# Linear attention feeding a two-layer network on one core: the opening reordered, and the attention of batches 3 to 7 computed with tokens on partitions and transposed by DMA

## The chip, the cores and the metric

The kernel runs on one core of a Trainium2 chip. The metric is device time in microseconds (us), the median of several executions. A profiled execution has a "span", which is about 1.7 us shorter than its time. Engines: PE is TensorE's matmul, PEld its weight load, DVE VectorE, ACT ScalarE, POOL GpSimd, SP SyncE; SPq is a DMA issue on SP. PSUM is the memory that matmuls write their results to; "regrouped" means copied so that all heads of a token lie together.

## The reference

```python
kv  = einsum('bhsd,bhse->bhde', k, v)            # 8 batches, 8 heads, 576 tokens, head size 64
out = einsum('bhsd,bhde->bhse', q, kv)
rms = sqrt(mean(out * out, axis=-1, keepdims=True) + 1e-6)
x   = (out / rms * g_norm)                       # -> 4608 tokens x 512
h   = x @ w_in                                   # 512 x 2048
g   = maximum(h, 0) + alpha * minimum(h, 0)
y   = g @ w_out                                  # 2048 x 512, float32 out
```

## The kernel before

The 4608 tokens are processed in nine windows of 512. The kernel keeps x transposed (features on partitions, tokens in columns), because the first layer needs it so. For each batch and pair of heads j, four small steps make it: transposing q on TensorE, kv, ot, and the norm with a sum over partitions made by a matmul with a mask.

```python
def step_t(b, j, pool=(ps_s, "s")):
    qs = bufs[b % NBUF]["q"]                      # q regrouped to tokens x heads
    qt_ps = pool[0].tile([P, NT * P], FP16, name="qt_ps", tag=pool[1])
    for t in range(NT):
        nc.tensor.matmul(out=qt_ps[:, t * P:(t + 1) * P], lhsT=qs[:, t, 2 * j:2 * j + 2, :],
                         rhs=ident16[:], is_transpose=True, ...)
    ...
def step_ot(w, j):      # ot_ps[features of the pair, 512 tokens] = kv^T q^T; then ACT squares it
def step_ssq(w, j):
    ot_ps, sq = ots.pop((w, j))
    ssq_ps = ps_q.tile([P, W], FP32, name="ssq_ps", tag="q")
    nc.tensor.matmul(out=ssq_ps[:], lhsT=mask16[:], rhs=sq[:], start=True, stop=True)
    # ACT: rstd = exp(-0.5 * ln(ssq / 64 + eps)), two passes of 128x512
    # DVE: xt = ot_ps * g * rstd
```

A window runs its first layer in 16 groups of four matmuls. Four second-layer matmuls of the window before follow each group, and then attention steps of the window after, spread over the groups:

```python
for w in range(1, NW):
    steps = window_steps(w + 1) if w + 1 < NW else []
    ...
    if 1 < w and w + 2 < B:
        load_batch(w + 2)                         # POOL issues six DMAs, fp32 to fp16
        regroup_batch(w + 2)                      # POOL copies to tokens x heads
    for g in range(NF):
        ...
        m1_group(w, g)                            # four matmuls h, then ACT Relu, DVE gt
        ...                                       # four matmuls y of window w - 1
        want = n * (g - first_g + 1) // (NF - 2 - first_g)
        while steps and n - len(steps) < want:
            steps.pop(0)()
```

Everything is scheduled by hand: each engine executes its instructions in the order in which this program emits them. That includes SP, which issues DMAs.

## Time and profile before

| | before |
|---|---|
| time | 329.71 us median (329.23 to 330.53) |
| span | 328.0 us |
| first first-layer matmul of window 2 | 90.0 us |
| from there to the end | 238.0 us |
| DMA packets under 512 B | 14,304 |

The clock row, the DMA totals, the queue that SP issues on, and the output stores are in the page of before (packets, MB, share of 16 engines; for the issue the last number is the median us to landing):

```profile
PEclk9999999798999999999999999999999999999999
...
DMA packets 47621, 28.07 MB, mean 86 GB/s; under 512 B 14304, under 2 KB 42992, under 8 KB 47600
...
q1 hardware_dynamic: 5696, 9.45, 10.2%
...
out_dram<-y_sb SPq DMA_DIRECT2D x40, 128.0 KB, 2.3
```

The clock is full after slice 10 (each slice is 8.2 us), and SP's queue carries little besides the output, 9.44 MB.

### The profile page before, as it was taken

The page shows a single profiled execution, that of the slowest core. Times are in us where ns is not written, and L with a number is a line of the kernel's source. Part 1 is how long each engine was busy: PE and PEld are TensorE (multiplying, and loading weights), DVE is VectorE, ACT ScalarE, POOL GpSimd, SP SyncE. Part 2 cuts the span into 40 slices and gives each one's busy share as a digit, 9 for nine tenths or more (in the row PEclk, how much of TensorE's full clock was granted, in tenths as well). Part 3 has the DMA queues.
Part 4 walks back from the last instruction along what each step waited for, and adds up shares of the span by engine and source line. Part 5 has one row for each costly group of instructions (what it writes and reads, how often), then busy time and mean ns, then how long its engine had stood idle before and what let it go on. Part 6 is the DMA issues. An engine that isn't in the chain of part 4 may idle for free.

```text
span 328.0 us, 4205 instructions
## 1 busy us (share of the span) xinstructions
PE 298.4 (91%) x1593; PEld 143.7 (44%) x1593; DVE 160.2 (49%) x271; ACT 173.4 (53%) x291; POOL 74.7 (23%) x80
## 2 busy tenths in 40 slices
PE   5657998768799999999999999999999999999994
PEld 1323354234355545544555455445544444444441
DVE  4247833285665545555455545554555455444300
ACT  2366605635846564657456745674557576544311
POOL 9723442765542055105500000000000000000000
PEclk9999999798999999999999999999999999999999
DMA  7999999996391199109901111101000211000132
GB/s 95 193 203 202 198 195 191 223 145 83 38 178 33 34 126 154 34 33 149 134 32 34 32 32 34 51 13 53 36 23 21 59 38 34 32 32 34 44 86 64
DMA packets 47621, 28.07 MB, mean 86 GB/s; under 512 B 14304, under 2 KB 42992, under 8 KB 47600
## 3 DMA queue, kind: packets, MB, share of 16 engines
q0 software_dynamic: 41904, 18.35, 44.5%
q1 hardware_dynamic: 5696, 9.45, 10.2%
q8 instruction: 12, 0.20, 0.3%
q14 instruction: 9, 0.07, 0.1%
HBM read 36.71 MB, written 9.44 MB: 141 GB/s over the span
## 4 chain that ended last, share of the span: by engine, by line
PE 83%; ACT 7%; DVE 4%; DMA 2%; issue 1%; POOL 1%; POOLq 0%; ACTq 0%
PE h_ps L300 36%; PE y_ps L322 34%; PE kv_ps L237 3%; PE ssq_ps L268 2%; PE qt_ps L222 2%; PE ot_ps L256 2%; ACT rstd L270 2%; DMA qsb<-in_q_dram 2%; ACT rstd L273 2%; DVE xt L275 1%; DVE gt L309 1%; ACT sq_sb L262 1%; ACT m_sb L307 1%; PE yd L322 1%; DVE qt_sb L231 1%
## 5 line engine op out<-in xcount | busy, mean ns | idle before, releaser
L300 PE MATMUL h_ps<-xt,w_in_sb 128*128 128x512 f16 x576 | 147.3, 384 | 4.1 <-ACT y_sb L329 1.5
L309 DVE SCALAR_TENSOR_TENSOR gt<-m_sb,beta_sb,h_ps 128x512 f16<-128x512 f32 x144 | 106.8, 745 | 88.4 <-ACT m_sb L307 86.9
L307 ACT ACTIVATE m_sb<-h_ps 128x512 f32<-128x512 f32 x144 | 85.1, 593 | 83.7 <-PE h_ps L300 83.6
L322 PE MATMUL y_ps<-w_out_sb,gt 128*128 128x512 f16 x512 | 128.8, 379 | 0.0
L322 PEld LDWEIGHTS <-gt 128*128 128x128 f16 x576 | 56.0, 98 | 67.5 <-issue 2.3
L300 PEld LDWEIGHTS <-w_in_sb 128*128 128x128 f16 x576 | 54.9, 99 | 67.2 <-issue 14.5
L275 DVE SCALAR_TENSOR_TENSOR xt<-ot_ps,g2col,rstd 128x512 f16<-128x512 f32 x36 | 27.0, 751 | 46.5 <-ACT rstd L273 46.5
L270 ACT ACTIVATE rstd<-ssq_ps,eps_t 128x512 f32<-128x512 f32 x36 | 24.7, 686 | 18.2 <-PE ssq_ps L268 18.2
L262 ACT ACTIVATE sq_sb<-ot_ps 128x512 f16<-128x512 f32 x36 | 21.3, 597 | 22.6 <-PE ot_ps L256 22.1
L329 ACT COPY y_sb<-y_ps 128x512 f32<-128x512 f32 x32 | 18.7, 585 | 18.4 <-PE y_ps L322 18.4
L273 ACT ACTIVATE rstd<-rstd 128x512 f32<-128x512 f32 x36 | 22.7, 629 | 1.1
L268 PE MATMUL ssq_ps<-sq_sb,mask 128*128 128x512 f16 x36 | 13.6, 378 | 7.0 <-ACT sq_sb L262 5.5
L222 PE MATMUL qt_ps<-ident,qsb 128*128 128x128 f16 x160 | 14.8, 227 | 5.7 <-DVE qsb L139 4.8
L237 PE MATMUL kv_ps<-vsb,ksb 128*128 128x128 f16 x160 | 14.5, 226 | 4.7 <-DVE qt_sb L231 4.7
L222 PEld LDWEIGHTS <-qsb 128*128 128x128 f16 x160 | 11.8, 101 | 13.5 <-DVE qsb L139 5.9
L231 DVE COPY qt_sb<-qt_ps 128x576 f16<-128x576 f16 x32 | 14.3, 451 | 6.4 <-PE qt_ps L222 6.3
L237 PEld LDWEIGHTS <-ksb 128*128 128x128 f16 x160 | 11.9, 101 | 12.1 <-issue 6.1
L256 PE MATMUL ot_ps<-qt_sb,kv_sb 128*128 128x512 f16 (+7 forms) x64 | 14.2, 296 | 0.3 <-DVE kv_sb L245 0.3
L128 POOL DMA_DIRECT2D ksb<-in_k_dram x8 | 5.6, 700 | 36.4 <-PE kv_ps L237 27.8
L139 POOL COPY ksb<-kst 128x2048 f16<-128x2048 f16 x5 | 9.5, 1893 | 18.7 <-DMA kst<-in_k_dram 18.7
L139 POOL COPY qsb<-qst 128x2048 f16<-128x2048 f16 x5 | 9.5, 1894 | 7.4 <-DMA qst<-in_q_dram 7.4
L139 POOL COPY vsb<-vst 128x2048 f16<-128x2048 f16 x5 | 9.5, 1894 | 6.8 <-DMA vst<-in_v_dram 6.8
(44 smaller groups left out, 111.6 us busy)
## 6 DMA issues: line engine op xcount, KB each, us to landing
out_dram<-y_sb SPq DMA_DIRECT2D x40, 128.0 KB, 2.3
out_dram<-y_sb SPq DMA_DIRECT2D x16, 256.0 KB, 2.3
kst<-in_k_dram POOLq DMA_DIRECT2D x7, 512.0 KB, 8.6
vst<-in_v_dram POOLq DMA_DIRECT2D x7, 512.0 KB, 10.1
qst<-in_q_dram POOLq DMA_DIRECT2D x7, 512.0 KB, 12.0
w_in_sb<-in_moe_w_in_dram POOLq DMA_DIRECT2D x4, 512.0 KB, 10.9
w_out_sb<-in_moe_w_out_dram POOLq DMA_DIRECT2D x4, 512.0 KB, 16.5
kst<-in_k_dram POOLq DMA_DIRECT2D x2, 256.0 KB, 5.5
```

The lines of the kernel that those rows point to most:

```text
L139: (eng or nc.vector).tensor_copy(out=dst, in_=src)
L222: nc.tensor.matmul(out=qt_ps[:, t * P : (t + 1) * P], lhsT=qs[:, t, 2 * j : 2 * j + 2, :], rhs=ident16[:], is_transpose=True, start=(t == ...
L237: nc.tensor.matmul(out=kv_ps[:], lhsT=ks[:, t, 2 * j : 2 * j + 2, :], rhs=vs[:, t, 2 * j : 2 * j + 2, :], start=(t == 0), stop=(t == NT - 1),)
L256: nc.tensor.matmul(out=ot_ps[:, n0 - w * W : n1 - w * W], lhsT=kvs[b, j][:], rhs=qts[b, j][:, n0 - b * S : n1 - b * S], start=True, stop=True,
L262: nc.scalar.activation(out=sq[:], in_=ot_ps[:], func=AF.Square)
L270: nc.scalar.activation(out=rstd[:], in_=ssq_ps[:], func=AF.Ln, bias=eps_t[:], scale=inv_d,)
L273: nc.scalar.activation(out=rstd[:], in_=rstd[:], func=AF.Exp, bias=0.0, scale=-0.5)
L275: nc.vector.scalar_tensor_tensor(out=xts[w, j][:], in0=ot_ps[:], scalar=g2col[:], in1=rstd[:], op0=ALU.mult, op1=ALU.mult,)
L300: nc.tensor.matmul(out=h_ps[:], lhsT=w_in_blk(c, g), rhs=xts[w, c][:], start=(c == 0), stop=(c == NC - 1),)
L307: nc.scalar.activation(out=m_sb[:], in_=h_ps[:], func=AF.Relu, scale=-1.0)
L309: nc.vector.scalar_tensor_tensor(out=gt[:], in0=m_sb[:], scalar=beta_sb[:, g : g + 1], in1=h_ps[:], op0=ALU.mult, op1=ALU.add,)
L322: nc.tensor.matmul(out=y[:], lhsT=gts[w, g][:, a * P : (a + 1) * P], rhs=w_out_blk(g), start=(g == 0), stop=(g == NF - 1),)
```

## The change

The intent has two parts. Part 1 shortens the opening: v is used as it was loaded instead of being regrouped, the loads and copies of batch 0 are reordered, and window 1's attention starts earlier. Part 2 takes work off TensorE from batch 3 on: a DMA transposes q straight from the regrouped buffer, a tile of 128 tokens times all eight heads is computed with tokens on partitions (so that the norm is a short VectorE reduction), and a second DMA transposes the finished x rows. The core of the diff:

```diff
+    NB_PE = 3
@@ part 1 (cut)
+    for nm, src in (("q", q), ("k", k), ("v", v)):           # remainder of batch 0, now on SP
+        nc.sync.dma_start(out=rem0[nm][0:REM], in_=src[0, :, MAIN:S, :]...)
     alpha_row = ...; nc.sync.dma_start(out=alpha_row[:], ...)
-        for nm in ("k", "v", "q"):
+        for nm in ("k", "q"):
             regroup(b, nm, 0, H, nc.gpsimd)
+            if nm == "v" and t < TPP:
+                return stages[b, nm][:, 2 * j : 2 * j + 2, t, :]
@@ part 2
+    def transpose_q(b):
+        qtms[b] = attn_p.tile([P, NT * NPAIR, P], FP16, name="qtm")
+        nc.sync.dma_start_transpose(out=qtms[b][:], in_=bufs[b % NBUF]["q"][:]...)
+    def tile_a(b, t):      # 4 matmuls of 128 columns: otm_ps = q kv; ACT squares
+        ot_ps = ps_o.tile([P, H, D], FP32, name="otm_ps", tag=f"o{n_tile[0] % 3}")
+    def tile_b(b, t):      # DVE sums over each head
+    def tile_c(b, t):      # ACT ln, exp on 128x8; POOL rg = rstd * g
+    def tile_d(b, t):
+        nc.vector.tensor_mul(out=x[0:n], in0=ot_ps[0:n], in1=rg[0:n])
+        nc.sync.dma_start_transpose(out=xm(w)[:, :, c : c + m], in_=x[i : i + m]...)
@@ the window loop
+            if g == NF - 3 and max(w + 2, NB_PE) < B and w + 2 >= NB_PE:
+                transpose_q(w + 2)

             want = n * (g - first_g + 1) // (NF - 2 - first_g)
             while steps and n - len(steps) < want:      # the last tile_d's come out of here
```

At group 13 of a window, q's transpose for the batch after next is therefore emitted just ahead of the tiles' last steps, on the same queue.

More of the change, by code (lines that the diff above doesn't have):

```diff
@@ L48 @@
     inv_d = 1.0 / D
+    NB_PE = 3
     const_p = ctx.enter_context(tc.tile_pool(name="constp", bufs=1))
     w_p = ctx.enter_context(tc.tile_pool(name="weights", bufs=1))
-    xt_p = ctx.enter_context(tc.tile_pool(name="xt", bufs=3))
+    xt_p = ctx.enter_context(tc.tile_pool(name="xt", bufs=2))
+    xm_p = ctx.enter_context(tc.tile_pool(name="xm", bufs=3))
     qkv_p = ctx.enter_context(tc.tile_pool(name="qkv", bufs=1))
@@ L60 @@
     ps_s = ctx.enter_context(tc.tile_pool(name="pss", bufs=1, space=bass.MemoryType.PSUM))
-    ps_o = ctx.enter_context(tc.tile_pool(name="pso", bufs=2, space=bass.MemoryType.PSUM))
-    ps_q = ctx.enter_context(tc.tile_pool(name="psq", bufs=1, space=bass.MemoryType.PSUM))
+    ps_o = ctx.enter_context(tc.tile_pool(name="pso", bufs=1, space=bass.MemoryType.PSUM))
     ctx.enter_context(
@@ L95 @@
     nc.vector.memset(warm16[:], 0.5)
+    rem0 = {}
+    for nm, src in (("q", q), ("k", k), ("v", v)):
+        rem0[nm] = ysb_p.tile([P, H, D], FP32, name=f"rem0{nm}", tag="y_sb")
+        nc.sync.dma_start(
+            out=rem0[nm][0:REM], in_=src[0, :, MAIN:S, :].rearrange("h s d -> s h d"),
+        )
     alpha_row = const_p.tile([NF, P], FP32, name="alpha_row")
     nc.sync.dma_start(out=alpha_row[:], in_=moe_alpha[:].rearrange("(g p) -> g p", p=P))
+    g_all = const_p.tile([P, D], FP32, name="g_all")
+    nc.sync.dma_start(out=g_all[:], in_=g_norm[:].partition_broadcast(P))
     g2col = const_p.tile([P, 1], FP32, name="g2col")
@@ L111 @@
         for nm in ("k", "v", "q"):
-            t[nm] = qkv_p.tile([P, NT, H, D], FP16, name=f"{nm}sb{i}")
-            nc.vector.memset(t[nm][REM:P, TPP, :, :], 0.0)
+            n = 1 if nm == "v" else NT
+            t[nm] = qkv_p.tile([P, n, H, D], FP16, name=f"{nm}sb{i}")
+            nc.vector.memset(t[nm][REM:P, n - 1, :, :], 0.0)
         bufs.append(t)
@@ L128, in load_rem @@
         nc.gpsimd.dma_start(
-            out=bufs[b % NBUF][nm][0:REM, TPP, :, :],
+            out=bufs[b % NBUF][nm][0:REM, 0 if nm == "v" else TPP, :, :],
             in_=srcs[nm][b, :, MAIN:S, :].rearrange("h s d -> s h d"),
@@ L179, in w_out_blk @@
         return w_out_sb[i][:, r, :]
-    for nm in ("k", "v", "q"):
-        load_main(0, nm, 0, H // 2)
-    for nm in ("k", "v", "q"):
-        load_rem(0, nm)
-    for nm in ("k", "v", "q"):
-        load_main(0, nm, H // 2, H)
+    for h0 in (0, H // 2):
+        for nm in ("q", "k", "v"):
+            load_main(0, nm, h0, h0 + H // 2)
     for i in range(WQ):
         load_w_in(i)
-    load_batch(1, ("k",))
+    load_batch(1, ("k", "q"))
     load_w_out(0)
-    load_w_out(1)
-    load_batch(1, ("v", "q"))
-    load_w_out(2)
-    load_w_out(3)
+    load_batch(1, ("v",))
+    for i in range(1, WQ):
+        load_w_out(i)
     load_batch(2)
     def keep_warm(n):
-        ps = ps_y.tile([P, W], FP32, name="warm_ps", tag="y")
+        ps = ps_s.tile([P, W], FP32, name="warm_ps", tag="s")
         for i in range(n):
@@ L216, with pair_cols, f @@
     qts, kvs, xts = {}, {}, {}
+    def pair_cols(b, nm, j):
+        def f(t):
+            if nm == "v" and t < TPP:
+                return stages[b, nm][:, 2 * j : 2 * j + 2, t, :]
+            if nm == "v":
+                return bufs[b % NBUF][nm][:, 0, 2 * j : 2 * j + 2, :]
+            return bufs[b % NBUF][nm][:, t, 2 * j : 2 * j + 2, :]
+        return f
     def step_t(b, j, pool=(ps_s, "s")):
-        qs = bufs[b % NBUF]["q"]
+        qs = pair_cols(b, "q", j)
         qt_ps = pool[0].tile([P, NT * P], FP16, name="qt_ps", tag=pool[1])
@@ L223, in step_t @@
                 out=qt_ps[:, t * P : (t + 1) * P],
-                lhsT=qs[:, t, 2 * j : 2 * j + 2, :],
+                lhsT=qs(t),
                 rhs=ident16[:],
@@ L233, in step_kv @@
     def step_kv(b, j, pool=(ps_s, "s")):
-        ks, vs = bufs[b % NBUF]["k"], bufs[b % NBUF]["v"]
+        ks, vs = pair_cols(b, "k", j), pair_cols(b, "v", j)
         kv_ps = pool[0].tile([P, P], FP32, name="kv_ps", tag=pool[1])
@@ L238, in step_kv @@
                 out=kv_ps[:],
-                lhsT=ks[:, t, 2 * j : 2 * j + 2, :],
-                rhs=vs[:, t, 2 * j : 2 * j + 2, :],
+                lhsT=ks(t),
+                rhs=vs(t),
                 start=(t == 0),
@@ L248, with xt_of, step_ot @@
     ots = {}
-    def step_ot(w, j):
-        ot_ps = ps_o.tile([P, W], FP32, name="ot_ps", tag="o")
+    xms = {}
+    def xt_of(w, c):
+        return xms[w][:, c, :] if w >= NB_PE else xts[w, c][:]
+    def step_ot(w, j, pool=None):
+        if pool is not None:
+            ot_ps = pool[0].tile([P, W], FP32, name="ot_ps", tag=pool[1])
+        else:
+            ot_ps = ps_o.tile([P, W], FP32, name="ot_ps", tag=f"o{j % 2}")
         n0 = w * W
@@ L265, in step_ssq, with ssq_mm @@
     def step_ssq(w, j):
+        ssq_mm(w, j)
+        norm(w, j)
+    def ssq_mm(w, j):
         ot_ps, sq = ots.pop((w, j))
-        ssq_ps = ps_q.tile([P, W], FP32, name="ssq_ps", tag="q")
+        ssq_ps = ps_o.tile([P, W], FP32, name="ssq_ps", tag="o2")
         nc.tensor.matmul(out=ssq_ps[:], lhsT=mask16[:], rhs=sq[:], start=True, stop=True)
@@ L273, in step_ssq, with norm @@
         nc.scalar.activation(out=rstd[:], in_=rstd[:], func=AF.Exp, bias=0.0, scale=-0.5)
+        ots[w, j] = (ot_ps, rstd)
+    def norm(w, j):
+        ot_ps, rstd = ots.pop((w, j))
         xts[w, j] = xt_p.tile([P, W], FP16, name="xt", tag=f"xt{j}")
@@ L278, in step_ssq, with step_tail_ot @@
         )
+    TAIL = NB_PE * (S - W)
+    JT = min(NPAIR, W // TAIL)
+    def step_tail_ot(i):
+        ot_ps = ps_o.tile([P, JT, TAIL], FP32, name="ot_ps", tag=f"o{i % 2}")
+        for u in range(JT):
+            j = i * JT + u
+            nc.tensor.matmul(
+                out=ot_ps[:, u, :], lhsT=kvs[NB_PE - 1, j][:],
+                rhs=qts[NB_PE - 1, j][:, S - TAIL : S], start=True, stop=True,
+            )
+        sq = attn_p.tile([P, JT, TAIL], FP16, name="sq_sb")
+        nc.scalar.activation(out=sq[:], in_=ot_ps[:], func=AF.Square)
+        ots["tail", i] = (ot_ps, sq)
@@ new lines, in step_tail_ssq @@
+    def step_tail_ssq(i):
+        ot_ps, sq = ots.pop(("tail", i))
+        ssq_ps = ps_o.tile([P, JT, TAIL], FP32, name="ssq_ps", tag="o2")
+        nc.tensor.matmul(out=ssq_ps[:], lhsT=mask16[:], rhs=sq[:], start=True, stop=True)
+        rstd = attn_p.tile([P, JT, TAIL], FP32, name="rstd")
+        nc.scalar.activation(
+            out=rstd[:], in_=ssq_ps[:], func=AF.Ln, bias=eps_t[:], scale=inv_d,
+        )
+        nc.scalar.activation(out=rstd[:], in_=rstd[:], func=AF.Exp, bias=0.0, scale=-0.5)
+        nc.vector.scalar_tensor_tensor(
+            out=xm(NB_PE)[:, i * JT : (i + 1) * JT, 0:TAIL], in0=ot_ps[:], scalar=g2col[:],
+            in1=rstd[:], op0=ALU.mult, op1=ALU.mult,
+        )
@@ new lines, with xm @@
+    qtms, tiles = {}, {}
+    def xm(w):
+        if w not in xms:
+            xms[w] = xm_p.tile([P, NPAIR, W], FP16, name="xm")
+        return xms[w]
+    def transpose_q(b):
+        qtms[b] = attn_p.tile([P, NT * NPAIR, P], FP16, name="qtm")
+        nc.sync.dma_start_transpose(
+            out=qtms[b][:], in_=bufs[b % NBUF]["q"][:].rearrange("p t h d -> p (t h d)"),
+        )
+    n_tile = [0]
+    def tile_a(b, t):
+        ot_ps = ps_o.tile([P, H, D], FP32, name="otm_ps", tag=f"o{n_tile[0] % 3}")
+        n_tile[0] += 1
+        for j in range(NPAIR):
+            nc.tensor.matmul(
+                out=ot_ps[:, 2 * j : 2 * j + 2, :], lhsT=qtms[b][:, t * NPAIR + j, :],
+                rhs=kvs[b, j][:], start=True, stop=True,
+            )
+        n = P if t < TPP else REM
+        sq = attn_p.tile([P, H, D], FP32, name="sqm_sb", tag="rstd")
+        nc.scalar.activation(out=sq[0:n], in_=ot_ps[0:n], func=AF.Square)
+        tiles[b, t] = [n, ot_ps, sq]
@@ new lines, in tile_b @@
+    def tile_b(b, t):
+        n, _, sq = tiles[b, t]
+        ss = attn_p.tile([P, H], FP32, name="ss", bufs=3)
+        nc.vector.tensor_reduce(
+            out=ss[0:n], in_=sq[0:n], op=ALU.add, axis=mybir.AxisListType.X,
+        )
+        tiles[b, t][2] = ss
+    def tile_c(b, t):
+        n, _, ss = tiles[b, t]
+        nc.scalar.activation(
+            out=ss[0:n], in_=ss[0:n], func=AF.Ln, bias=eps_t[0:n], scale=inv_d,
+        )
+        nc.scalar.activation(out=ss[0:n], in_=ss[0:n], func=AF.Exp, bias=0.0, scale=-0.5)
+        rg = attn_p.tile([P, H, D], FP32, name="rg")
+        nc.gpsimd.tensor_tensor(
+            out=rg[0:n], in0=ss[0:n].unsqueeze(2).to_broadcast([n, H, D]),
+            in1=g_all[0:n].unsqueeze(1).to_broadcast([n, H, D]), op=ALU.mult,
+        )
+        tiles[b, t][2] = rg
@@ new lines, in tile_d, with phase_steps @@
+    def tile_d(b, t):
+        n, ot_ps, rg = tiles.pop((b, t))
+        x = attn_p.tile([P, H, D], FP16, name="xrow", bufs=3)
+        nc.vector.tensor_mul(out=x[0:n], in0=ot_ps[0:n], in1=rg[0:n])
+        i = 0
+        while i < n:
+            w, c = divmod(b * S + t * P + i, W)
+            m = min(n - i, W - c)
+            nc.sync.dma_start_transpose(
+                out=xm(w)[:, :, c : c + m], in_=x[i : i + m].rearrange("p h d -> p (h d)"),
+            )
+            i += m
+    def phase_steps(w):
+        if w < NB_PE:
+            return window_steps(w)
+        if w >= NW:
+            return []
+        todo = [(b, t) for b in range(NB_PE, min(B, w + 1)) for t in range(NT)
+                if (b, t) not in done and b * S + t * P < (w + 1) * W]
+        done.update(todo)
+        old = [x for x in todo if x[0] < w]
+        new = [x for x in todo if x[0] == w]
+        pre = []
+        if w == NB_PE:
+            n = NPAIR // JT
+            pre = [lambda i=i: step_tail_ot(i) for i in range(n)] + [
+                lambda i=i: step_tail_ssq(i) for i in range(n)]
+        kv = [lambda j=j: step_kv(w, j) for j in range(NPAIR)] if w < B else []
+        first = []
+        for i in range(max(len(pre), len(kv))):
+            first += kv[i : i + 1] + pre[i : i + 1]
+        seq = old + new
+        lead = len(old)
+        steps = []
+        if lead == 0:
+            steps += [[f] for f in first]
+            first = []
+        for i in range(len(seq) + 3):
+            m = []
+            for k, fn in ((3, tile_d), (0, tile_a), (1, tile_b), (2, tile_c)):
+                if 0 <= i - k < len(seq):
+                    m.append(lambda fn=fn, x=seq[i - k]: fn(*x))
+            if i < lead:
+                cut = -(-len(first) // (lead - i))
+                m += first[:cut]
+                first = first[cut:]
+            steps.append(m)
+        return [lambda m=m: [f() for f in m] for m in steps]
@@ L280, in window_steps @@
+    done = set()
     def window_steps(w):
@@ L300, in m1_mm @@
             nc.tensor.matmul(
-                out=h_ps[:], lhsT=w_in_blk(c, g), rhs=xts[w, c][:],
+                out=h_ps[:], lhsT=w_in_blk(c, g), rhs=xt_of(w, c),
                 start=(c == 0), stop=(c == NC - 1),
@@ L345 @@
     H_POOL = (ps_h, "h")
-    for j0 in (0, 2):
-        regroup(0, "q", 2 * j0, 2 * j0 + 4)
-        regroup(0, "v", 2 * j0, 2 * j0 + 4, nc.scalar)
-        regroup(0, "k", 2 * j0, 2 * j0 + 4)
-        j1 = j0 + 1
-        step_t(0, j0, H_POOL)
-        step_t(0, j1, H_POOL)
-        step_kv(0, j0)
-        step_kv(0, j1, H_POOL)
-        step_ot(0, j0)
-        step_ot(0, j1)
-        if j0 == 0:
-            keep_warm(4)
-            step_ssq(0, j0)
-            step_ssq(0, j1)
-            keep_warm(6)
+    for nm in ("q", "k", "v"):
+        nc.scalar.copy(out=bufs[0][nm][0:REM, 0 if nm == "v" else TPP, :, :], in_=rem0[nm][0:REM])
+    regroup(0, "q", 0, H // 2)
+    step_t(0, 0, H_POOL)
+    regroup(0, "k", 0, H // 2)
+    step_t(0, 1, H_POOL)
+    keep_warm(3)
+    step_kv(0, 0)
+    step_kv(0, 1, H_POOL)
+    step_ot(0, 0)
+    step_ot(0, 1)
+    regroup(0, "q", H // 2, H)
+    step_t(0, 2, H_POOL)
+    regroup(0, "k", H // 2, H)
+    step_t(0, 3, H_POOL)
+    ssq_mm(0, 0)
+    ssq_mm(0, 1)
+    norm(0, 0)
+    step_kv(0, 2)
+    step_kv(0, 3, H_POOL)
+    norm(0, 1)
+    step_ot(0, 2)
+    step_ot(0, 3, (ps_y, "y"))
     first = [ps_h.tile([P, W], FP32, name="h_ps", tag="h") for g in range(3)]
@@ L365 @@
     step_ssq(0, 2)
+    keep_warm(2)
     step_ssq(0, 3)
@@ L373 @@
         m1_group(0, g)
-    for nm in ("q", "k", "v"):
-        regroup(1, nm, 0, H)
+        if g == 10:
+            regroup(1, "k", 0, H)
+        if g == 14:
+            regroup(1, "q", 0, H)
+    AHEAD = 3
     ys = [
@@ L381 @@
         ps_h.tile([P, W], FP32, name="yc", tag="h"),
-        ps_h.tile([P, W], FP32, name="yd", tag="h"),
     ]
     steps = window_steps(1)
+    n = len(steps)
     for g in range(NF):
-        for a in range(TPW):
+        for a in range(AHEAD):
             y_mm(ys[a], 0, a, g)
-            if g >= 6 and steps and (a == 1 or (a == 3 and g >= 8)):
+            if a != 1 and steps and n - len(steps) < n * (AHEAD * g + a + 1) // (AHEAD * (NF - 3)):
                 steps.pop(0)()
-    for a in range(TPW):
+    for a in range(AHEAD):
         y_out(ys[a], 0, a)
-    for f in steps:
-        f()
+    regroup_batch(2)
     for w in range(1, NW):
-        steps = window_steps(w + 1) if w + 1 < NW else []
+        steps = phase_steps(w + 1)
         n = len(steps)
@@ L404 @@
             if w == 1 and g == first_g - 1:
-                for nm in ("q", "k", "v"):
-                    regroup(2, nm, 0, H)
                 load_batch(3)
@@ L409 @@
             m1_group(w, g)
-            if w > 1:
+            if w == 1:
+                if g == 0:
+                    y = ps_y.tile([P, W], FP32, name="y_ps", tag="y")
+                y_mm(y, 0, AHEAD, g)
+                if g == NF - 1:
+                    y_out(y, 0, AHEAD)
+            else:
                 a, part = divmod(g, TPW)
```

## The prediction

> **What bounds the kernel now.** I read the summary of engines first, then the slices of the span, the busy time by stretch, TensorE's waits, and the timeline of TensorE instruction by instruction.
>
> From the page (engines, then 40 slices of 8.2 us each, tenths of busy time):
>
> ```profile
> PE 298.4 (91%) x1593; PEld 143.7 (44%) x1593; DVE 160.2 (49%) x271; ACT 173.4 (53%) x291; POOL 74.7 (23%) x80
> ...
> PE   5657998768799999999999999999999999999994
> ...
> DMA  7999999996391199109901111101000211000132
> GB/s 95 193 203 202 198 195 191 223 145 83 38 178 33 34 126 154 34 33 149 134 32 34 32 32 34 51 13 53 36 23 21 59 38 34 32 32 34 44 86 64
> ```
>
> There are two regimes. In the first eleven slices (to about 90 us) TensorE has holes and the DMA engines are full: they load weights and batches 0 to 3. After that TensorE is full and the DMA engines are mostly free. The stretches say it in microseconds (start:end, length, busy time of each engine, clock, DMA, GB/s):
>
> ```profile
> 0.00:9.87 9.87, 4.64 (x11) 1.56 (x12) 4.35 (x19) 2.33 (x2) 8.34 (x17) 1.00 0.99 106
> 9.87:39.00 29.13, 23.27 (x122) 11.21 (x123) 16.95 (x29) 16.91 (x28) 13.59 (x18) 1.00 1.38 200
> 39.00:62.40 23.40, 18.84 (x118) 9.37 (x116) 9.11 (x17) 9.11 (x17) 9.34 (x9) 1.00 1.49 190
> 62.40:90.00 27.60, 21.92 (x116) 10.43 (x116) 17.04 (x29) 16.15 (x30) 16.54 (x16) 0.88 0.77 112
> 90.00:308.50 218.50, 215.07 (x1162) 104.71 (x1161) 111.96 (x178) 125.34 (x212) 26.91 (x22) 1.00 0.32 56
> ```
>
> Busy matmul time is not work, because matmuls overlap: the timeline shows four 512-column matmuls every 0.86 us, so one costs 0.216 us of TensorE, not the 0.38 us of its row; five 128-column ones cost 0.28 us, 0.056 each:
>
> ```profile
> 93.78 0.44 PE L237 MATMUL kv_ps<-vsb,ksb 128*128 128x128 f16 x5
> 94.06 1.03 PE L300 MATMUL h_ps<-xt,w_in_sb 128*128 128x512 f16 x4
> 94.92 1.03 PE L322 MATMUL y_ps<-w_out_sb,gt 128*128 128x512 f16 x4
> 95.79 0.44 PE L222 MATMUL qt_ps<-ident,qsb 128*128 128x128 f16 x5
> ...
> 118.82 0.38 PE L268 MATMUL ssq_ps<-sq_sb,mask 128*128 128x512 f16 x1 [0.69 <-ACT sq_sb L262]
> ```
>
> With these costs, window 2 starts at 90.0 us. From there remain 448 first-layer and 512 second-layer matmuls, 960 x 0.2158 = 207.2 us; attention of batches 3 to 7 at 20 transposes, 20 kv, and 4 + 4 wide matmuls each (2 x 1.11 + 8 x 0.216 = 3.95 us), plus 1.73 for the last window: 21.5 us; five stalls like the last line (0.84 us lost each), 4.2 us; and 4.8 us after the last matmul. Sum 237.7; the trace has 238.0. So TensorE alone bounds the last 238 us. Before 90 us there are only 192 x 0.216 + 3 x 4 = 53.4 us of TensorE work: 36.6 us are lost. TensorE's waits name where:
>
> ```profile
> PE ssq_ps L268 <- ACT sq_sb L262: 5.5, 7, 1.2
> PE qt_ps L222 <- DVE qsb L139: 4.8, 3, 2.9
> PE kv_ps L237 <- DVE qt_sb L231: 4.7, 5, 1.9
> ```
>
> qsb is the regrouped q: TensorE waits for data that has landed and is being rearranged by VectorE.
>
> **What the Trainium skill says.** "VectorE: DVE Perf Modes", The three transpose paths, gives 1309 ns for one 128x128 transpose by DMA and 390 ns on TensorE. The trace puts a TensorE transpose at 0.056 us in a stream, so the move saves little per tile. "DMA: Bandwidth & Descriptors", Latency and other measured facts, gives 261 GB/s for a DMA transpose with a non-contiguous middle dimension; no transpose of this kind is in the trace. The same page, Issuing engines are not separate DMA queues, says that all queues share 16 engines; in the trace the output stores' time to landing runs from 2.0 through a median of 2.3 to 5.7 us, which fits sharing but doesn't prove it. "GPSIMD Engine Reference", 3.1, has 4497 ns for a two-input operation of 2048 elements; from it I estimate 1.2 us for the 512-element one added here; the trace has only copies (1.89 us for 2048 f16).
>
> **Part 1, the opening.** Removed: regrouping v everywhere (kv reads the staged v with strides); the remainder loads of batch 0 leave POOL's queue; the second half of q and k no longer stands behind the norm of the first half on VectorE; window 1's attention starts with the first y matmul, not at g = 6; a quarter of window 0's y moves into window 1. Working: before, the half batches have landed by 9.4 (q) and 14.9 us, yet the second half's q copy ran at 18.4 because it stood behind the norm; first-layer matmuls began at 20.9 and 26.0. Unblocked, I put those at 17.5 (w_in's first quarter landed at about 17.4, from POOL's queue waits) and 22.1: 3.5 us gained. Window 0's first layer ends at 36 instead of 39, less 0.7 for two regroupings on VectorE among its evacuations. Then y with three columns: 48 x 0.216 + 4.0 attention + 1.5 of stalls, to 52; before, four columns ended at 60.6, and the next window began at 62.5. Window 1: 80 x 0.216 + 4.0 + 3.5 of stalls = 24.8, against 27.6 before for 64. So window 2 starts at about **77.5** instead of 90.0. The bytes and their order hardly change; the arrival times of w_out (30, 31, 42, 45 us before) and of batch 2 (near 54) still fit.
>
> **Part 2, tokens on partitions, batches 3 to 7.** Removed from TensorE: 100 transposes (5.6 us), 24 wide ssq (5.2), 24 wide ot (5.2), five stalls (4.2). Added: 100 ot matmuls of 128 columns (25 tiles of 4; 5.6 us), the tail of batch 2 (0.65). kv stays. Net 238 - 14 = 223.9 us from window 2 to the end, if nothing new waits. ACT loses two passes of 0.63 to 0.69 us per pair; VectorE gains a reduction per tile; both are at half load and not the bound.
>
> What is added on the path, from the built order of instructions:
> - Three PSUM buffers hold the tiles, and the fourth tile of a window waits for tile_d of the first, which on VectorE stands behind this group's gt. From lines like those above: the group ends at 95.09, Relu to 95.72, gt to 96.50, tile_d 0.7 more to 97.2, while TensorE is ready at 95.79: 1.4 us. Windows with 4, 5, 4, 5, 4 tiles have 1 + 2 + 1 + 2 + 1 = 7 such waits: **9.8 us**.
> - The next window's first matmul needs all its xm. The last tile_d ends 2.1 us after group 13's end, and TensorE arrives 4.15 us after it. A transpose DMA as quick as the stores (2.3) lands at 4.4: 0.3 us, six times. But the q transpose (655 KB; 2.5 us at 261 GB/s, an estimate from that page) stands just before it in SP's queue in four windows; in two of them it is issued one group later, and x waits 1.2. Sum **3.5 us** if the page's rate holds. If it runs twice as long, these four lose 3 to 5 us each: about 20 us.
> - POOL's product stands behind the load and regrouping of a batch (14.3 + 1.9 us, from 64.68 to 80.8): free 11 to 14 us into a window, needed at 13 to 14. **1 us**.
>
> Sum with the quick transposes: 77.5 + 223.9 + 14.3 = 315.7 us of span, 317.4 with the 1.7 us between span and time. With slow ones about 332.
>
> **The rivals.** (1) The transposes are hidden and only the opening and 14 us of TensorE work count: 77.5 + 223.9 + 1.7 = 303; against it are the built order's waits, which I don't see how to avoid. (2) The DMA transpose takes the bound: 1309 ns each one after the other would be 26 us for 20 tiles, over 50 us per batch with x, more than a window's 32 us; then time goes above 345. For it: no trace of this case shows its speed; against: the page's rate. (3) The wait moves from regrouped q to DMA arrival in the opening, and only 5 us of 12.5 are gained: the DMA row is 9 there; against it, copies started well after landing. Then 325.
>
> **Range and chances.** Quick transposes (half), about 317; moderately slow (a third), 324 to 332; very slow (a sixth), above. The opening adds 3 us either way. I choose 320.5 us, between the first two and nearer the first, range 310 to 335; 323.1 and 336.3 are the 2% borders, so 0.55, 0.33 and 0.12.
>
> **What would show it.** Window 2's first matmul near 77.5 us; qt_ps waiting for qsb under 2 us in all; TensorE from window 3 on without 128-column transposes; otm_ps waiting for xrow seven times at 1.4 us; h_ps waiting for the DMA of xm six times at a window's start, longest where qtm was issued just before; POOL's rg near 1.2 us. The prediction is wrong if xm's landing takes above 5 us, if rg holds VectorE and so gt, or if the clock row falls below 9 at the window starts.

## The result, and the profile after

| | before | after |
|---|---|---|
| time, median | 329.47 us (328.71 to 330.53, 4 runs) | 358.90 us (356.84 to 361.32, 4 runs) |
| ratio | | 1.089, 95% interval 1.082 to 1.097 |
| window 2 starts | 90.0 us | 80.3 us |
| from there to the end | 238.0 us | 276.3 us |

Ratios here are the mean time of one kernel's runs over that of the other's runs of the same rounds, so they are not quite the ratio of the medians that are quoted. Executions over 1.5% slower than the fastest of the same kernel are left out of the means.

The kernel is 8.9% slower. The opening is 9.7 us shorter as intended, and 38.3 us are lost after it. The page of after:

```profile
PE 291.6 (82%) x1526; PEld 137.1 (38%) x1526; DVE 164.8 (46%) x275; ACT 156.7 (44%) x301; POOL 93.1 (26%) x99
...
PE   4759979889994198874989419999979998999994
...
PEclk9999999999998589996999858999999999999999
DMA  7999997969329921199112992145014212210033
...
DMA packets 73141, 34.53 MB, mean 97 GB/s; under 512 B 39824, under 2 KB 68512, under 8 KB 73120
...
q1 hardware_dynamic: 32800, 16.11, 22.2%
```

Slices are 8.9 us now. TensorE's row has three new holes (the digits 41, 74 and 41), and the clock row drops below 9 at or just after each of them. Read the DMA row against them: two 9s stand at each hole. The transposes move 6.2 MB (five q of 655 KB and 2.9 MB of x) in about 25,500 new packets of under 512 B, so some 244 B each.

TensorE's waits of after name the holes (us in total, times, longest):

```profile
PE h_ps L464 <- DMA xm<-xrow: 32.6, 3, 12.6
PE otm_ps L361 <- DVE xrow L394: 8.7, 7, 1.3
...
PE kv_ps L252 <- DVE kv_sb L260: 2.0, 4, 0.9
```

The first line is new and big: the first layer waits for the transposed x at the start of windows 3, 4 and 5. The matmuls themselves, on TensorE's timeline around the first one:

```profile
109.75 1.03 PE L486 MATMUL y_ps<-w_out_sb,gt 128*128 128x512 f16 x4
123.39 1.86 PE L464 MATMUL h_ps<-xm,w_in_sb 128*128 128x512 f16 x4 [12.61 <-DMA xm<-xrow]
125.05 1.91 PE L486 MATMUL y_ps<-w_out_sb,gt 128*128 128x512 f16 x4
126.75 1.44 PE L464 MATMUL h_ps<-xm,w_in_sb 128*128 128x512 f16 x4
```

Four matmuls start every 1.66 to 1.70 us after the wait instead of every 0.86, because TensorE's clock had gone down meanwhile: some 0.42 us each. Such matmuls are called cold below. By the starts, the three long waits cost another 2.1, 1.4 and 1.6 us in cold matmuls. The Trainium skill, "TensorE: Matmul & The Clock Gate", Part 1, puts the cold state at half clock after an idle window of about 3.4 us and a 512-column matmul at 426.7 ns cold and 215.7 warm; the spacing in this trace agrees, and the idle times here, 7.4 us and more, are longer than that window.

SP's timeline shows what x stands behind:

```profile
105.72 2.56 SPq L399 DMA_TRANSPOSE xm<-xrow  x2
108.38 6.51 SPq L351 DMA_TRANSPOSE qtm<-qsb  x1
114.98 2.74 SPq L399 DMA_TRANSPOSE xm<-xrow  x2
```

The same trace has this transpose once with no load beside it, at the end of window 5:

```profile
242.09 2.60 SPq L351 DMA_TRANSPOSE qtm<-qsb  x1
```

SP is held 6.51 us by the issue of q's transpose instead of 2.60. Only then can it issue the last two transposes of x, and the first of those lands after 8.27 us, where the median of all 28 is 2.4. The chain of work that ended last has it:

```profile
114.98 8.27 DMA xm<-xrow
```

The load is on POOL's timeline, from 1 us before q's transpose:

```profile
107.35 0.74 POOL L138 DMA_DIRECT2D ksb<-in_k_dram  x1
```

This is the first of the six transfers of batch 5 (3.5 MB of float32 read), which POOL issues as soon as it is through with its last product of window 3's tiles. The stretches of the three waits (start:end, length, busy us of PE, PEld, DVE, ACT, POOL, then clock, DMA share, GB/s):

```profile
110.78:123.39 12.61, 0.00 (x1) 0.03 (x2) 0.55 (x1) 0.58 (x1) 3.22 (x3) 0.62 1.37 165
...
158.20:165.65 7.45, 0.02 (x1) 0.00 (x0) 0.57 (x1) 0.58 (x1) 1.89 (x2) 0.74 1.47 167
200.50:213.07 12.57, 0.00 (x0) 0.03 (x1) 0.53 (x1) 0.58 (x1) 2.70 (x2) 0.59 1.42 164
```

TensorE does nothing, and the others little. The DMA share (time of all packets that start in the stretch, over 16 engines, so it can exceed 1) reads as in the opening (1.38 and 1.49 in the prediction's stretches), where the loads fill it.

The account from window 2 on: 223.9 (the prediction's TensorE work with tail) + 34.8 lost at window starts (32.6 in the three long waits; the rest is in the short ones and in the time until the next start) + 9.9 lost around the seven otm_ps waits (8.7 by the view) + 2.7 around the kv_ps waits + 5.1 of cold matmuls = 276.4. The trace has 276.3.

### The profile page after: what moved, and what is told of

It reads as the page before. It is cut to its first block, busy times and chain, and to the rows that moved or that the text cites. A ratio compares the mean times of both kernels' runs of the same rounds, so it can differ in the third digit from the quotient of the medians.

```text
span 356.6 us, 4212 instructions
## 1 busy us (share of the span) xinstructions
PE 291.6 (82%) x1526; PEld 137.1 (38%) x1526; DVE 164.8 (46%) x275; ACT 156.7 (44%) x301; POOL 93.1 (26%) x99
## 3 DMA queue, kind: packets, MB, share of 16 engines
q1 hardware_dynamic: 32800, 16.11, 22.2%
## 4 chain that ended last, share of the span: by engine, by line
PE 68%; DMA 11%; ACT 6%; DVE 6%; SPq 4%; issue 3%; POOL 1%; POOLq 0%; ACTq 0%
PE h_ps L464 33%; PE y_ps L486 28%; DMA xm<-xrow 7%; SPq L351 4%; DMA w_in_sb<-in_moe_w_in_dram 4%; ACT m_sb L471 3%; DVE gt L473 2%; PE kv_ps L252 2%; PE otm_ps L361 2%; DVE xrow L394 1%; ACT rstd L296 1%; DVE xt L305 1%; ACT rstd L299 1%; PE ssq_ps L294 1%; PE yc L486 1%
## 5 line engine op out<-in xcount | busy, mean ns | idle before, releaser
L464 PE MATMUL h_ps<-xm,w_in_sb 128*128 128x512 f16 x384 | 101.5, 388 | 33.8 <-DMA xm<-xrow 32.6
L385 POOL TENSOR_TENSOR rg<-ss,g_all 128x512 f32<-128x512 f32 (+1 forms) x25 | 26.0, 1040 | 124.6 <-ACT ss L383 84.6
L464 PE MATMUL h_ps<-xt,w_in_sb 128*128 128x512 f16 x192 | 47.5, 379 | 3.2 <-DVE xt L305 1.5
L367 ACT ACTIVATE sqm_sb<-otm_ps 128x512 f32<-128x512 f32 (+1 forms) x25 | 14.9, 597 | 16.7 <-PE otm_ps L361 16.7
L149 POOL COPY qsb<-qst 128x2048 f16<-128x2048 f16 x6 | 11.4, 1894 | 37.6 <-DMA qst<-in_q_dram 33.3
L394 DVE TENSOR_TENSOR xrow<-otm_ps,rg 128x512 f16<-128x512 f32 (+1 forms) x25 | 17.0, 682 | 0.0
L373 DVE TENSOR_REDUCE ss<-sqm_sb 128x8 f32<-128x512 f32 (+1 forms) x25 | 16.9, 675 | 0.0
L252 PE MATMUL kv_ps<-vst,ksb 128*128 128x128 f16 x128 | 12.6, 224 | 4.2 <-DVE kv_sb L260 2.0
L305 DVE SCALAR_TENSOR_TENSOR xt<-ot_ps,g2col,rstd 128x512 f16<-128x512 f32 x12 | 9.0, 751 | 14.7 <-ACT rstd L299 14.6
L361 PEld LDWEIGHTS <-qtm 128*128 128x128 f16 x100 | 7.2, 98 | 16.2 <-issue 6.8
L296 ACT ACTIVATE rstd<-ssq_ps,eps_t 128x512 f32<-128x512 f32 x12 | 8.2, 684 | 7.0 <-PE ssq_ps L294 6.9
L284 ACT ACTIVATE sq_sb<-ot_ps 128x512 f16<-128x512 f32 x12 | 6.9, 592 | 9.9 <-PE ot_ps L278 9.9
```

The source lines that it names most:

```text
L149: (eng or nc.vector).tensor_copy(out=dst, in_=src)
L252: nc.tensor.matmul(out=kv_ps[:], lhsT=ks(t), rhs=vs(t), start=(t == 0), stop=(t == NT - 1),)
L361: nc.tensor.matmul(out=ot_ps[:, 2 * j : 2 * j + 2, :], lhsT=qtms[b][:, t * NPAIR + j, :], rhs=kvs[b, j][:], start=True, stop=True,)
L367: nc.scalar.activation(out=sq[0:n], in_=ot_ps[0:n], func=AF.Square)
L373: nc.vector.tensor_reduce(out=ss[0:n], in_=sq[0:n], op=ALU.add, axis=mybir.AxisListType.X,)
L385: nc.gpsimd.tensor_tensor(out=rg[0:n], in0=ss[0:n].unsqueeze(2).to_broadcast([n, H, D]), in1=g_all[0:n].unsqueeze(1).to_broadcast([n, H, D ...
```

## The experiments

The theory: x arrives late for two reasons that make each other worse. **Order**: q's transpose is ahead of x in SP's queue. **Contention**: the load of a batch starts at the same moment, and transposes are slow beside it. Rival theories: DMA transposes are slow in themselves; the time is lost to the tiles' in-window waits or to the opening; or only one of the two reasons matters.

All timed experiments were compared with the kernel before on the same chip (330.1 to 330.2 us median in the first two jobs, 329.5 in the third). The table lists the wait ahead of the first first-layer matmul of windows 3 to 6, as TensorE's timeline shows it; "-" where there is none. Under some of them the view names gt or nothing as the releaser, though the same x is wanted.

| version | time, us | ratio to before | waits at windows 3, 4, 5, 6 |
|---|---|---|---|
| after | 358.90 | 1.089 | 12.61, 7.43, 12.59, 0.86 |
| e_open: part 1 alone | 320.34 | 0.973 | (no transposes) |
| e_xfirst: x ahead of q | 344.45 | 1.043 | 5.92, 5.88, 6.20, 0.23 |
| e_noload: three loads left out | 330.04 (1 run) | | 2.54, 0.84, 3.44, 0.78 |
| e_gate: loads held back | 345.04 | 1.047 | 3.10, 4.61, 3.46, 4.93 |
| e_gate_xfirst: both | 322.33 | 0.976 | 0.18, 0.19, 0.68, 0.22 |
| e_extra: one more load | 375.31 (1 run) | | 13.39, 7.66, 13.94, 12.25 |
| e_early: x product earlier | 329.90 | 0.998 | 6.17, 2.79, 3.03, - |
| f_all: all three | 314.60 | 0.952 | 0.76, -, 0.69, - |
| f_alpha: f_all and alpha's load first | 313.03 | 0.951 | 0.77, -, 0.67, - |

### e_open: the opening alone

```diff
-    NB_PE = 3
+    NB_PE = NW
-    JT = min(NPAIR, W // TAIL)
+    JT = max(1, min(NPAIR, W // TAIL))
```

> Only the reordered opening; all nine windows keep the normalisation and the transposes on TensorE. Theory (the loss of the full change is the DMA transposes beside the batch load, the opening itself gains): window 2 starts near 80 us as in the full change and the rest is as before, so about 329.5 - 9.7 = 320 us. Rival (the reordered opening pushes later loads into a bad place and costs as well): 326 us or more, with new waits for qsb or kst after 90 us.

Measured: 320.34 us (319.91 to 322.73), ratio 0.973 (0.967 to 0.978). The longest entry in TensorE's waits is the old one, ssq_ps for sq_sb, 5.6 us in seven times. Window 2 starts at 80.8 us, and 238.0 us follow to the end of the span of 318.8, as before. So part 1 gives its gain in full, and part 2 costs the difference of 38.6 us to after's 358.9. The rival "the opening" falls.

### e_xfirst: x ahead of q in SP's queue

```diff
-            if g == NF - 3 and max(w + 2, NB_PE) < B and w + 2 >= NB_PE:
-                transpose_q(w + 2)
             want = ...
             while steps and n - len(steps) < want:
                 steps.pop(0)()
+            if g == NF - 3 and max(w + 2, NB_PE) < B and w + 2 >= NB_PE:
+                transpose_q(w + 2)
```

> The full change with the q transpose of the next batch issued behind the last x transposes of a window instead of ahead of them. Rival (place in the queue: x waits because SP is busy 6.5 us with the q transpose): the three waits for xm of 12.6, 7.4 and 12.6 us vanish, about 325 us. Theory (the transposes are slowed by the batch load that runs on the same 16 DMA engines): x lands still late, each of the three waits stays at 3 us or more, and the time is between 335 and 350 us.

Measured: 344.45 us (343.07 to 344.85), ratio 1.043 (1.038 to 1.049). SP's timeline, then the first matmul of window 3:

```profile
105.46 5.55 SPq L399 DMA_TRANSPOSE xm<-xrow  x4
111.11 8.63 SPq L351 DMA_TRANSPOSE qtm<-qsb  x1
```

```profile
116.45 1.86 PE L464 MATMUL h_ps<-xm,w_in_sb 128*128 128x512 f16 x4 [5.92 <-DMA xm<-xrow]
```

All four x transposes are issued by 111.0, and TensorE still waits until 116.45: the order explains half of this wait, and x beside the load is slow even when it is first. The last two transposes land 8.1 and 8.2 us after their issue, where e_noload below has 2.3 for the same two. The three long waits fell from 32.6 to 18.0. q's transpose, now wholly under the load, landed after 15.5 us (median of five).

### e_noload: no loads at three window ends

```diff
-            load_batch(w + 2)
+            if w == 2:
+                load_batch(w + 2)
+            else:
+                for nm in ("k", "v", "q"):
+                    stages[w + 2, nm] = stages[w, nm]
```

The result is wrong for batches 5 to 7, which reuse older data; the order of all queues stays.

> Wrong result on purpose: the loads of the staged values of batches 5 to 7 and of their remainders are left out (the arithmetic runs on what is in the buffers). Theory (contention): like the delayed load or a little better, span about 318 to 322, each wait for xm below 2 us. Rival (transposes slow by themselves): three waits of 7 to 12 us as in the full change.

Measured: 330.04 us once, span 328.3. The same two places:

```profile
109.64 2.40 SPq L351 DMA_TRANSPOSE qtm<-qsb  x1
```

```profile
114.57 1.02 PE L464 MATMUL h_ps<-xm,w_in_sb 128*128 128x512 f16 x4 [2.54 <-DMA xm<-xrow]
```

q's transpose holds SP for 2.40 us and lands after 4.2 us (median; 9.3 in after). So the transpose is not slow in itself, and that rival falls. The time missed the expectation by some 8 us, mostly because I had not counted that order alone still costs 2.54 + 0.84 + 3.44 + 0.78 = 7.6 us. The wait is long in windows 3 and 5, where the last two x transposes stand behind q's, and short in windows 4 and 6, where only one does.

### e_gate: loads held back to the next window

```diff
+        gated = 2 < w and w + 2 < B
-        if 1 < w and w + 2 < B:
+        if 1 < w and w + 2 < B and not gated:
             load_batch(w + 2); regroup_batch(w + 2)
+            if gated and g == 1:                      # POOL waits for gt of group 1
+                gt1 = const_p.tile([P, 1], FP16, name=f"gate{w}")
+                nc.gpsimd.tensor_copy(out=gt1[:], in_=gts[w, 1][:, 0:1])
+                load_batch(w + 2)
+            if gated and g == 12:
+                regroup_batch(w + 2)
```

> The full change, order on SP unchanged, but the loads of batches 5 to 7 start only after group 1 of their window, when the last x transposes have landed (a one-column copy on POOL that reads gt of group 1 holds them back). Theory (contention with the load): the q transpose takes about 2.6 us of SP as at the one window end without a load, the three waits for xm fall below 2 us each, the clock dips go, and the time falls by 30 to 37 us to about 322. Rival (place in the queue alone, or transposes slow by themselves): the waits stay at 7 us or more, time above 345.

Measured: 345.04 us (344.03 to 347.08), ratio 1.047 (1.041 to 1.052), far from what I expected. The contention is gone: at the ends of windows 2 to 5, q's transpose holds SP for 2.95 to 3.04 us, and it lands after 5.0 (median). But my edit brought a new delay. Moved to group 12, POOL's copy of q ends only at 147.35 us in window 3, q's transpose is issued at 147.38, and x stands behind it; the wait of window 4 is 4.61 us where e_noload has 0.84, that of window 6 is 4.93 where it has 0.78. This run alone therefore doesn't settle the size of the contention; the next one does.

### e_gate_xfirst: both reasons removed

The two edits together.

> Both mendings of the window end: the load held back to group 1 and the q transpose behind x. Theory (the waits for xm come from the load and from the place in the queue, and from nothing else): all waits for xm below 1 us, clock dips gone; from the full change 32.6 us of waits, 5 us of cold matmuls: about 320 us, so the same as the opening alone. Rival (transposes cost more than their queue and the load): waits of 2 us or more stay, 328 us or more.

Measured: 322.33 us (322.04 to 322.76), ratio 0.976 (0.973 to 0.978). Window 3 starts so:

```profile
112.60 1.02 PE L464 MATMUL h_ps<-xm,w_in_sb 128*128 128x512 f16 x4 [0.18 <-DMA xm<-xrow]
```

With q behind x it no longer matters that q comes late. The four runs make a square. Sum of the four waits: 33.5 us with both causes (after), 18.2 with the load alone (e_xfirst), 7.6 with the order alone (e_noload), 1.3 with neither. The single causes add 16.9 and 6.3 to that 1.3; together they add 32.2, 8.9 more than their sum. That is x standing behind a q transpose that the load has slowed: at the ends of windows 2 and 4 its issue holds SP for 6.5 and 6.8 us in after, and for 2.4 and 2.6 in e_noload, and the difference, 8.3 us, is nearly all of the 8.9. Both causes are needed to explain these waits, and a third is not (e_early will show that they also shrink when x is issued earlier). (The two halves of the square without contention differ a little: e_noload leaves the loads out, e_gate_xfirst issues them later.)

What remains is informative: window 2 starts at 81.9 in this run, and 239.1 us follow, more than before's 238.0. With x hardly late, part 2 still gains nothing, because what is lost around its seven otm_ps waits (9.9 us, as in after), its four kv_ps waits (2.7) and six window starts (2.6) eats its 14 us: 223.9 + 15.2 = 239.1.

### e_extra: a load beside the one quick q transpose

```diff
+        if w == 6:
+            for nm in ("k", "v", "q"):
+                st = stage_p.tile([P, H, TPP, D], FP16, name=f"{nm}st", tag=f"{nm}st")
+                nc.gpsimd.dma_start(out=st[:]..., in_=srcs[nm][7, :, 0:MAIN, :]...)
```

> The full change with one more load of 1.5 MB (a batch's staged k, v and q once more, into buffers that are free) put where the batch load stands in the earlier windows, at the end of window 5, where the full change has a q transpose but no load and lost only 0.9 us. Theory (contention with the load): h_ps at the start of window 6 now waits 7 to 13 us for xm, the span grows by 8 to 14 us to 365 to 371. Rival (something of windows 2 to 4 other than the load): that wait stays below 2 us, span as in the full change, 357.

Measured: 375.31 us once, span 373.5 against 356.6. In after, window 6 started with a wait of 0.86. Here, on SP's and TensorE's timelines:

```profile
246.09 6.36 SPq L351 DMA_TRANSPOSE qtm<-qsb  x1
```

```profile
262.70 1.87 PE L464 MATMUL h_ps<-xm,w_in_sb 128*128 128x512 f16 x4 [12.25 <-issue]
```

A load put beside the undisturbed q transpose makes a wait of the same size as the other two: 6.36 us of SP instead of 2.60, 12.25 us of wait instead of 0.86. The effect can be switched on as well as off. The span grew by 16.9, more than expected; 11.4 are the new wait, 2.4 the other three waits, which are longer in this run (13.39, 7.66, 13.94), 2.7 more cold matmuls, and 0.4 the opening (window 2 at 80.7). What lengthened the other three waits is open.

### e_early: the product that frees PSUM ahead of the group's evacuation

tile_d (the product that writes xrow, frees the PSUM tile and issues x's transpose) is emitted before m1_group instead of after it, so on VectorE it no longer stands behind the group's gt.

```diff
-            for k, fn in ((3, tile_d), (0, tile_a), (1, tile_b), (2, tile_c)):
+            early.append([lambda x=seq[i - 3]: tile_d(*x)] if 0 <= i - 3 < len(seq) else [])
+            for k, fn in ((0, tile_a), (1, tile_b), (2, tile_c)):
@@ (cut) in the window loop, before m1_group(w, g), when a step falls due
+                for f in ea[n - len(steps)]:
+                    f()
```

> The full change with the product that makes xrow emitted ahead of the group's own matmuls and evacuation, not behind them; nothing else. Theory (seven waits of tile_a for a buffer, each 1.4 us, because xrow stands behind gt on VectorE): these seven vanish, 9.8 us less, and x is ready 1.5 to 2 us earlier at six window ends; about 345 us. Rival (the buffer wait is hidden behind the other stalls): 355 us or more.

Measured: 329.90 us (327.39 to 331.63), ratio 0.998 (0.991 to 1.005): 29 us better than after, where I expected 14. TensorE's waits:

```profile
PE h_ps L469 <- DMA xm<-xrow: 12.0, 3, 6.2
...
PE otm_ps L361 <- DVE xrow L394: 2.0, 2, 1.0
```

The otm_ps waits fell by 6.7 us as the theory of the in-order VectorE has it. The rest came from x: issued earlier, x gets ahead of q's transpose and partly ahead of the load. On SP's timeline of window 2's end, three x transposes run from 109.77 and q's only follows at 113.95, as if e_xfirst's edit had been made; and the wait of window 3, 6.17 us, is e_xfirst's 5.92.

### f_all: the three edits together

> All three: load held back, q transpose behind x, xrow ahead of gt. Theory: window 2 at 80 us, 223.9 us of work from there, 3 to 5 us of small waits, 1.7 us outside the span: 309 to 311 us, faster than the opening alone (320) by about 3%. Rival (tokens on partitions have a further cost that the mended waits hid): 318 us or more.

Measured: 314.60 us (314.01 to 315.36), ratio 0.952 (0.949 to 0.956), 3.6 us above the upper end of what I expected. Half of that is in the window part: 230.8 us from window 2 to the end, where 223.9 and 3 to 5 of small waits were expected. The other half is in the opening. Window 2 starts at 82.0, 1.7 us later than in after: TensorE waited 3.0 us for alpha (2.35 in after), and its matmuls start 0.22 us apart only from 22.2 us on, in after from about 15. The clock view gives 0.71 of full for the first 20 us and 1.00 for after, and the expectation of f_alpha rests on that, but this 1.00 is not a full clock: the trace of after has no record of the clock before 14.9 us, and its 512-column matmuls start 0.43 us apart until 11.5. The same opening also varies from run to run: window 2 starts between 80.1 (e_xfirst) and 82.6 us (f_all_r).

### f_alpha and f_all_r: alpha's load first

Alpha's 8 KB load stands behind the three remainder loads that part 1 put on SP. f_alpha moves it ahead of them; f_all_r is f_all again, on the same chip.

```diff
+    alpha_row = ...; nc.sync.dma_start(out=alpha_row[:], ...)
     rem0 = {}
     for nm, src in (("q", q), ("k", k), ("v", v)): ...
-    alpha_row = ...; nc.sync.dma_start(out=alpha_row[:], ...)
```

> The combined version with one line moved: the load of alpha (8 KB) is issued by SP ahead of the three remainder loads of batch 0 instead of behind them. In the combined version's trace TensorE waits 3.0 us for alpha_row at 8.96 us, the granted clock over the first 20 us is 0.71, and first-layer matmuls begin at 20.1 us, where the changed kernel (2.35 us of that wait, clock 1.00) begins at 19.4. If that wait is what cools TensorE, it falls below 1.5 us, the clock over the first 20 us is 1.00, window 2 starts 1.0 to 2.0 us earlier than the 82 of the combined version, and the time is 312.5 to 313.8. Rival: the clock of the opening varies from run to run and the remainder loads then come later instead; the time stays at 314.5 within 0.7.

> The combined version once more, on the same chip as the one with alpha's load first, so that less than one per cent can be read: 314.6 within 0.6 as in its first run. If the clock of its opening is 1.00 this time, with the same 3 us wait, the wait is not what lowers it.

Measured: f_alpha 313.03 us (312.85 to 313.71, 5 runs), ratio 0.951 (0.948 to 0.954); f_all_r 314.28 (313.36 to 315.15, 6 runs), ratio 0.954 (0.951 to 0.957). By the medians f_alpha is 1.25 us better; the ranges overlap by 0.35 us, so the sign is likely and the size is rough. The wait for alpha is gone, but the clock view over the first 20 us says 0.77 (0.73 in f_all_r), not the 1.00 that I had wrongly taken for a full clock; matmuls start 0.22 us apart from 21.1 us on, and from 23.0 in f_all_r. The wait moved to the next arrival, v of batch 0, where TensorE waits 3.3 us (1.3 in f_all_r). First-layer matmuls begin at 19.5 instead of 20.5, and window 2 at 81.2 instead of 82.6, a start within the spread of the runs before.

f_alpha is the fastest version, 4.9% below before. Its page:

```profile
PE 286.4 (92%) x1526; PEld 137.1 (44%) x1526; DVE 165.6 (53%) x275; ACT 156.6 (50%) x301; POOL 93.2 (30%) x102
...
PEclk9669999999999999999999999999999999999999
```

And its waits of TensorE from 82 us on:

```profile
PE otm_ps L361 <- DVE xrow L394: 2.1, 2, 1.1
PE kv_ps L252 <- DVE kv_sb L260: 2.0, 4, 0.9
PE h_ps L469 <- DMA xm<-xrow: 0.8, 1, 0.8
PE h_ps L469 <- DVE gt L478: 0.7, 1, 0.7
```

Window 2 starts at 81.2 and 230.8 us follow: the predicted 223.9 of TensorE work, plus 2.4 lost around otm_ps, 2.7 around kv_ps and 1.5 at window starts, is 230.5.

## Why the prediction was wrong, point by point

- **The opening** was right in kind and nearly in size: 77.5 predicted, 80.3 measured in after and 80.8 in e_open. The working's own terms (36, then 16, then 24.8) add up to 76.8, not 77.5. Window 1 took its 24.7 us; window 0's first layer ended at 37.9 instead of 36, and its y part took 17.6 instead of 16. The first layer began at 19.4 instead of 17.5, just as w_in's first quarter landed, at 19.4 (17.1 in before), so the arrival order did matter; that is the third rival in a small way. The wait for alpha, which the change itself put behind three loads, was not foreseen. TensorE's waits for qsb are 0.8 us, under the 2 that was named.
- **TensorE's work of 223.9 us** was right. f_alpha, where almost every wait is gone, closes on it within 0.3 us.
- **Seven waits of tile_a at 1.4 us, 9.8 in all**, were right: seven times, 1.2 to 1.3 us by the view, 9.9 lost. e_early shows that the cause is the one named, the product behind gt on VectorE.
- **POOL's product** took 1.04 us; 1.2 had been estimated. No TensorE wait was put down to it.
- **The step that failed is "x at window ends", put at 3.5 us if the page's rate holds, about 20 if the transposes take twice as long.** It measured 33.5 us of waits and 5.1 us of cold matmuls behind them. The order in SP's queue had been seen, with the right four windows. What went wrong are two flight times, both taken as if the transposes ran alone. x was put at 2.3 us, as quick as the stores. It is that quick in e_noload, but in after it takes 7.3 to 8.9 us where a batch's load has just started, and with x first in the queue (e_xfirst) this alone leaves 18.2 us of waits. q's transpose was put at 2.5 us, or twice that. By itself it lands after 4.1 to 4.3 us, and with that the step would have cost 7.6 us (e_noload). Beside a load it takes 9 to 14 us in after, and holds SP for up to 6.8. The prediction had both facts: that all queues share the DMA engines, and that a load with its regrouping, 16 us long, is over 11 to 14 us into a window, so that it starts near the window's start. It used the load only as a delay of POOL's product and never set it beside the transposes. (Its sum for slow transposes, about 332, is a span; with the 1.7 us it is 334.)
- **The rivals.** "The DMA transpose takes the bound, above 345" gave the right region of time for a wrong reason: it supposed that each 128x128 transpose is slow by itself, and the quiet 4.1 us for 20 of them rule that out. "All hidden, 303" was refuted by the tile waits, as the prediction said. "Only 5 us of 12.5 gained in the opening" was refuted by 9.7.
- **Its own signs.** Of the three that would make it wrong two occurred: a landing of x above 5 us (7.3 to 8.9 measured) and the clock row below 9 at window starts (5, 6 and 8 in the row).
- **Not foreseen**: two kv steps that fall into one step share one PSUM bank and cost 2.7 us.

The change lost because its second part had a gain of 14 us to give, spent nearly 13 of it on two kinds of waits inside windows, and then put a DMA transpose on the path at the moment when a bulk load fills the DMA engines.

## What to carry to other kernels

When a DMA is put on the path that sets the end, list which other transfers start within its flight, on any queue, and what stands ahead of it in its own queue; a rate measured for it alone is not its time beside a bulk load. Hold the bulk load back until the short transfers have landed, and issue what is needed first ahead of what is needed a window later. On an engine that works in order, put the instruction that frees a scarce buffer ahead of the evacuation that can wait: here a few moved lines took 29 us off, because they also put x ahead of q's transpose and partly ahead of the load.

## What the Trainium skill lacked or had wrong

- **"DMA: Bandwidth & Descriptors", Latency and other measured facts**: it has 261 GB/s for a DMA transpose with a non-contiguous middle dimension (more for the contiguous case), and nothing on how long a transpose takes beside a load. By 261 GB/s 655 KB take 2.5 us, an estimate. Measured from issue to landing: 4.1 us quiet, 9 to 14 beside a 3.5 MB load in after, up to 16.2 in e_xfirst. The Queues, rings and completion order section says that each DMA engine takes turns between queues by packets; the transposes' packets are about 244 B, which may be why they lose so much to a load, but no run here varied the packet size.
- **The same page, Issuing engines are not separate DMA queues**: it calls the issuing sequencer's time usually small relative to the DMA itself. For transposes it is not: SP is held about 1.2 us for one of 128 x 512 that lands after 2.4, 2.4 to 2.6 us for q's that lands after 4.1 to 4.3, and 2.8 to 8.6 us for q's beside a load (2.79 and 6.78 in after). Everything behind it in SP's queue waits that long.
- **"VectorE: DVE Perf Modes", The three transpose paths**: 1309 ns for a 128x128 DMA transpose would be 26 us for q's 20 tiles one after the other; they took 4.1 us together, so 0.21 us each. Its 390 ns for TensorE is also far above 0.056 us in a stream. Read as the cost of each of many, the table would mislead a choice between the two.
- **"TensorE: Matmul & The Clock Gate", Part 1**: it has the clock go down after at least one idle window of about 3.4 us. Here waits of 2.79 and 3.03 us (e_early) already brought it down, as did 3.44 (e_noload) and 3.46 (e_gate), while 2.54 (e_noload) and 3.10 us (e_gate) left it up.
